# A Fourier-mixing layer and a feed-forward layer on one core: transposes through DRAM in four chunks on two queues, inverse twiddle matrices formed by TensorE, and a reordered start

## The chip, the cores and the metric

The kernel runs on one core of one Trainium2 chip. A core has TensorE (PE, matrix products into PSUM, with PEld for its weight loads), VectorE (DVE), ScalarE (ACT), GpSimd (POOL) and SyncE (SP). Here SP and POOL also issue the transfers: each has a queue that is served in order, so an issue that waits holds up everything behind it on that queue. All transfers are carried by the same 16 DMA engines. The metric is the device time of one execution in microseconds, and the number to compare is a median over runs.

## The reference

`x` has 8 batches of 3008 rows by 256 columns. Each batch is Fourier-transformed along its rows, multiplied by a complex filter, and transformed back. The result goes through a feed-forward layer of width 2048 with a leaky activation.

```python
batch, seq, dim = (8, 3008, 256)
X = np.fft.rfft(x, axis=1)
F = (filt_r + 1j * filt_i)[None, :, :]
y = np.fft.irfft(X * F, n=x.shape[1], axis=1)
...
h = x @ w_in                                      # x is now y as 24064 x 256; w_in is 256 x 2048
g = np.maximum(h, 0.0) + alpha * np.minimum(h, 0.0)
return (g @ w_out).astype(np.float32)             # w_out is 2048 x 256
```

## The kernel before

**The transform.** 3008 = 47 x 64, so the transform of a batch is done in two stages with a transpose between them, and the inverse likewise. Class `Fft` holds one batch:

- `piece_a` (16 per batch, L162): a 47-point transform of one piece of `x` (tile `xs`, loaded and cast by `load_x`, four chunks per batch, L120) by one 512-column matmul (L168); the PSUM result is copied to `asb`, by ACT (L250) or DVE (L253).
- `save_a` (4 per batch, L171) writes a quarter of `asb` to DRAM in runs of 4 KB. `turn_a` (L175), once per batch after the last save, reads it back into tile `at` with the other axis on partitions: four DMAs, each in runs of 512 bytes.
- `piece_b` (12 per batch, L184): two matmuls with matrix `twf_s` (L188), then two products on DVE with the filter, `uu` (L191) and `ww` (L192, with `filts_s`, a copy of the filter with its halves exchanged). `piece_b0` (L195) is the form for batch 0, with six matmuls and no need of `filts_s`.
- `piece_c` (12 per batch, L211): four matmuls with the inverse matrix `twi_s` (L220, L221), copied to tile `v`. `twi_s` is loaded from a constant in DRAM.
- `turn_c` (4 per batch, L224) writes a quarter of `v` to DRAM in runs of 512 bytes by four DMAs; the last call also reads all of it back into `zt` by four DMAs in runs of 4 KB.
- `piece_d` (16 per batch, L238): four matmuls (L243) and a copy into `yT`, the input of the feed-forward layer.

**The feed-forward layer.** The token axis is cut in blocks of 512 (one of 384 in every twelve). Class `Block` runs 16 steps per block. `up(j)` (L327) is two 512-column matmuls (L332) per step; after each odd step ACT copies two steps' worth from PSUM tile `hps` to `gt` (L337), and DVE finishes the activation with two scalings (`m`, L340) and one addition (L341). `down` (L344) runs for the block before: four 256-column matmuls per step (L350); ACT copies its sums to `osb` (L355), and SP stores them (L316).

**What sets the order.** Every engine's order is the order in which the program emits its instructions; nothing is reordered. First comes a prologue, in which batch 0 goes through stages a to d alone. Then a loop runs over steps, numbered from 0: `up`, `down` of the block before, and then the entries that `plan` holds for that step. Block 0 (steps 0 to 15) has no `down`. `plan_fft(b, a0, ga, ta, b0, gap, d0)` (L364) places the other batches' pieces: `piece_a` from step `a0`, every `ga` steps; `turn_a` at `ta`; `piece_b` from `b0`, every `gap` steps, with `piece_c` three steps behind it; `piece_d` from `d0`. All evictions of planned pieces are on ACT, but those of batch 0's `piece_d`, which alternate between ACT and DVE (L383).

**Buffers.** PSUM has two buffers of `hps`, two of `op` and two of `psF`; planned a, b, c and d pieces all take their bank from `psF` (function `bank`, L146). `at`, `asb`, `v` and `zt` have one buffer each, `xs` four.

**Queues before.** SP issues the constants, saves, turns and stores. POOL issues the transfers that cast: `x`, the filter, `w_in`, `w_out`. Two tiny copies into `gate` on POOL (L273, L293) hold `w_in` and `w_out` back until batch 0's `at` has landed, and the `x` of batch 1 (the second batch) until `zt` has.

Of the kernel before, what the change touches and what calls it, by code (L numbers as in the profile page):

```python
# [25 lines left out]
def _build_consts():  # L26

    s1 = np.arange(N1)
    s2 = np.arange(N2)
    k1 = np.arange(NK1)
    p = np.arange(64)
    k2 = np.where(p < 32, p, 95 - p)
    g = np.where(p < 32, 1.0, -1.0)

    a1 = 2 * np.pi * np.outer(s1, k1) / N1
    wf1 = np.zeros((2 * N1, 96))  # L40
    wi3 = np.zeros((96, 2 * N1))
    scale = np.where(k1 == 0, 1.0, 2.0) / NFFT
    for h in range(2):
        r = slice(h * N1, h * N1 + N1)
        wf1[r, h * 48 : h * 48 + NK1] = np.cos(a1)
        wf1[r, h * 48 + NK1 : h * 48 + 48] = -np.sin(a1)
        wi3[h * 48 : h * 48 + NK1, r] = (np.cos(a1) * scale).T
        wi3[h * 48 + NK1 : h * 48 + 48, r] = (-np.sin(a1) * scale).T
# [4 lines left out]
    twf = np.empty((128, NK1, 128))  # L53
    twf[:64, :, :64], twf[64:, :, :64] = c, s
    twf[:64, :, 64:], twf[64:, :, 64:] = -s * g, c * g
    ec, es = c.transpose(2, 1, 0), s.transpose(2, 1, 0)
    gp = g[:, None, None]
    twi = np.empty((128, NK1, 2, 128))
    twi[:64, :, 0, :64], twi[:64, :, 0, 64:] = ec, es
    twi[64:, :, 0] = -twi[:64, :, 0]  # L60
    twi[:64, :, 1, :64], twi[:64, :, 1, 64:] = -es * gp, ec * gp
    twi[64:, :, 1] = twi[:64, :, 1]
    return wf1, wi3, twf, twi


@with_exitstack
def kernel(
# [15 lines left out]
    twi_d = nc.inline_tensor(twi_np.astype(np.float16), name="c_twi")  # L83
# [29 lines left out]
    gate = konst.tile([128, 2], FP16, name="gate")  # L113
    yT = konst.tile([128, 2, 2 * NFFT], FP16, name="yT")

    def xrow(b, h, c):
# [35 lines left out]
    class Fft:  # L152
# [16 lines left out]
            evict(self.asb[:, 2 * i : 2 * i + 2].rearrange("p a d -> p (a d)"), ps[0:96])  # L169

        def save_a(self, c):  # L171
            s = slice(8 * c, 8 * c + 8)
            nc.sync.dma_start(out=a_dram[self.b, :, s], in_=self.asb[:, s])

        def turn_a(self, eng, ka=0, kb=NK1):  # L175
            for h in range(2):
                for c in range(2):
                    r = h * 48 + c * NK1
                    q = c * 64 + NH * h
                    eng.dma_start(  # L180
                        out=self.at[q : q + NH, ka:kb],
                        in_=a_dram[self.b, r + ka : r + kb].rearrange("k s d -> s k d"))
# [28 lines left out]
        def piece_c(self, kp, evict, pv=None):  # L211
# [9 lines left out]
                nc.tensor.matmul(pv[:, kh], twi_s[:, k1, 1], ww[:, kh], start=False, stop=True)  # L221
            evict(self.v[:, 2 * kp : 2 * kp + 2], pv)

        def turn_c(self, q):  # L224
            k = 6 * q
            for h in range(2):
                for c in range(2):
                    r = h * 48 + c * NK1 + k
                    p = c * 64 + NH * h
                    nc.sync.dma_start(  # L230
                        out=v_dram[self.b, r : r + 6].rearrange("k s d -> s k d"),
                        in_=self.v[p : p + NH, k : k + 6])
            if q == 3:
                for g in range(4):
                    s = slice(8 * g, 8 * g + 8)
                    nc.sync.dma_start(out=self.zt[:, s], in_=v_dram[self.b, :, s])
# [30 lines left out]
    nc.sync.dma_start(out=twi_s[:, 12:24], in_=twi_d.ap()[:, 12:24])  # L267
    nc.sync.dma_start(out=wi3_s, in_=wi3_d.ap())
    alp = psO.tile([128, 2, D], FP32, name="op")
    nc.tensor.transpose(alp[:, 0, 0:16], al16, id32)  # L270
    nc.vector.tensor_copy(al_s, alp[:, 0, 0:16])
    nc.gpsimd.tensor_scalar(alm_s, al_s, 1.0, -1.0, OP.mult, OP.add)
    nc.gpsimd.tensor_copy(gate[:, 0:1], f0.at[:, 11, 0:1])  # L273
    for kt in range(2):
        nc.gpsimd.dma_start(out=win_s[:, kt], in_=moe_w_in[kt * 128 : (kt + 1) * 128])
    for q in range(2):
# [4 lines left out]
    for kp in range(12):  # L281
        f0.piece_b0(kp)
        if kp >= 1:
            f0.piece_c(kp - 1, on_act, psO.tile([128, 2, D], FP32, name="op"))
        if kp >= 3 and kp % 3 == 0:
            f0.turn_c(kp // 3 - 1)
    f0.piece_c(11, on_act, psO.tile([128, 2, D], FP32, name="op"))
    f0.turn_c(3)
# [5 lines left out]
    for c in range(4):  # L294
        xc[(1, c)] = load_x(1, c)
    for i in range(4):
        f0.piece_d(i, both[i % 2], i % 2 == 1)

# [62 lines left out]
    def put(step, fn, *args):  # L361
        plan.setdefault(step, []).append((fn, args))

    def plan_fft(b, a0, ga, ta, b0, gap, d0):  # L364
        f = Fft(b)
        for i in range(16):
            put(a0 + ga * i, f.piece_a, i, on_act)
        for c in range(4):
            put(a0 + ga * (4 * c + 3), f.save_a, c)
            if b + 1 < NB:  # L370
                put(a0 + ga * (4 * c + 3) + 1,
                    lambda b=b, c=c: xc.update({(b + 1, c): load_x(b + 1, c)}))
# [62 lines left out]
```

## Time and profile before

| what | value |
|---|---|
| median of 3 runs | 861.59 us (860.19 to 862.68) |
| span of the profiled execution | 861.4 us |
| PE busy | 799.4 us (93%) |
| first 512-column matmul of batch 0's `piece_a` starts | 7.54 us |
| first matmul of `piece_b0` starts | 33.05 us |
| last matmul of batch 0's `piece_c` starts | 53.81 us |
| first matmul of `piece_d` starts | 63.08 us |
| step 0 / step 16 of the loop starts | 64.62 / 81.80 us |
| PE busy in 191.3 to 861.4 us | 657.3 of 670.1 us |

The profile shows for each engine what it did and what ended its idle time. A rows' "idle before" counts only where the engine sets the end; here that is PE for nearly all of the loop. The table says that PE has little to give after some 190 us: what it lacks to its span lies ahead of that.

### The profile page before, as it was taken

What the parts mean: (1) busy time and instruction counts of PE and PEld (TensorE: products, weight loads), DVE (VectorE), ACT (ScalarE), POOL (GpSimd) and SP (SyncE); (2) the same over time, 40 slices, a digit from 0 to 9 for tenths busy, and PEclk for the clock granted to TensorE, in tenths of its full rate; (3) what the DMA queues carried; (4) which work ended last, traced back from release to release, by engine and by line L of the source; (5) the groups of instructions that cost most, each with busy time, mean ns of one, the idle gap of its engine ahead of it and who ended that gap; (6) DMA issues with size and microseconds to landing.
All of it is one profiled execution on the core that took longest, in us unless ns stands there. A gap on an engine that the chain in (4) does not pass through costs nothing.

```text
span 861.4 us, 15404 instructions
## 1 busy us (share of the span) xinstructions
PE 799.4 (93%) x5809; PEld 541.7 (63%) x5809; DVE 612.9 (71%) x1361; ACT 586.6 (68%) x817; POOL 41.4 (5%) x85
## 2 busy tenths in 40 slices
PE   3458989979999999999999999999999999999997
PEld 1134556756666766676666766676666766676665
DVE  2246668758877787678877787778877788777773
ACT  2027757767787767777777767777777866677663
POOL 4103000000000000000000000000000000000000
PEclk9989989999999999999999999999999999999999
DMA  9989835761368224772268323682148122411111
GB/s 212 250 171 197 179 69 133 157 144 41 75 148 199 60 62 97 172 158 51 53 162 195 73 64 83 164 181 50 43 120 186 50 68 50 129 38 39 39 41 49
DMA packets 95378, 95.95 MB, mean 111 GB/s; under 512 B 8312, under 2 KB 85128, under 8 KB 95176
## 3 DMA queue, kind: packets, MB, share of 16 engines
q1 hardware_dynamic: 85448, 78.19, 35.8%
q0 software_dynamic: 8256, 16.00, 12.3%
q10 hardware_dynamic: 1600, 0.79, 0.5%
q8 instruction: 45, 0.74, 0.4%
q14 instruction: 29, 0.24, 0.1%
HBM read 59.55 MB, written 49.81 MB: 127 GB/s over the span
## 4 chain that ended last, share of the span: by engine, by line
PE 70%; DVE 13%; ACT 7%; DMA 6%; issue 2%; SPq 1%; POOL 0%; ACTq 0%; DVEq 0%; POOLq 0%
PE hps L332 29%; PE op L350 28%; ACT gt L337 6%; DVE gt L341 4%; DVE m L340 4%; PE psF L168 3%; DVE ww L192 3%; DVE uu L191 3%; PE psF L221 2%; DMA at<-a_dram 2%; PE psF L243 2%; DMA a_dram<-asb 2%; PE psF L220 1%; DMA xs<-in_x_dram 1%; PE psF L188 1%
## 5 line engine op out<-in xcount | busy, mean ns | idle before, releaser
L337 ACT ACTIVATE gt<-hps 128x1024 f16<-128x1024 f32 (+1 forms) x384 | 385.1, 1003 | 134.6 <-PE hps L332 134.1
L332 PE MATMUL hps<-yT,win_s 128*128 128x512 f16 (+1 forms) x1536 | 454.3, 377 | 1.1 <-ACT yT L250 1.0
L350 PE MATMUL op<-wout_s,gt 128*128 128x256 f16 x3008 | 453.3, 273 | 0.6 <-DVE gt L341 0.6
L350 PEld LDWEIGHTS <-gt 128*128 128x128 f16 x3008 | 294.4, 98 | 192.5 <-issue 2.8
L340 DVE TENSOR_SCALAR m<-gt,alm_s 128x512 f16<-128x512 f16 (+1 forms) x768 | 233.5, 346 | 164.1 <-ACT gt L337 162.8
L341 DVE TENSOR_TENSOR gt<-gt,m 128x1024 f16<-128x1024 f16 (+1 forms) x384 | 261.6, 681 | 24.3 <-DVE m L340 0.9
L332 PEld LDWEIGHTS <-win_s 128*128 128x128 f16 x1536 | 145.6, 98 | 31.6 <-issue 5.0
L250 ACT ACTIVATE asb<-psF 96x512 f16<-96x512 f32 x120 | 70.7, 593 | 40.2 <-PE psF L168 40.2
L250 ACT ACTIVATE v<-psF 128x512 f16<-128x512 f32 x84 | 50.2, 598 | 34.9 <-PE psF L221 34.9
L250 ACT ACTIVATE yT<-psF 128x376 f16<-128x376 f32 x120 | 58.1, 484 | 20.9 <-PE psF L243 20.7
L191 DVE TENSOR_TENSOR uu<-psF,filt_s 128x512 f16<-128x512 f32 x84 | 57.4, 683 | 6.7 <-PE psF L188 6.7
L355 ACT ACTIVATE osb<-op 128x512 f32<-128x512 f32 x96 | 56.3, 587 | 6.9 <-PE op L350 3.7
L168 PE MATMUL psF<-xs,wf_s 94*96 94x512 f16 x120 | 47.8, 398 | 11.0 <-DMA xs<-in_x_dram 8.3
L192 DVE TENSOR_TENSOR ww<-psF,filts_s 128x512 f16<-128x512 f32 x84 | 57.1, 679 | 0.0
L123 POOL DMA_DIRECT2D xs<-in_x_dram x64 | 32.9, 522 | 458.2 <-PE psF L168 457.1
L243 PE MATMUL psF<-wi_s,zt 96*128 96x94 f16 x504 | 42.7, 207 | 10.8 <-DMA zt<-v_dram 9.0
L243 PEld LDWEIGHTS <-zt 96*128 96x128 f16 x512 | 36.3, 100 | 18.9 <-DMA zt<-v_dram 9.3
L221 PE MATMUL psF<-ww,twi_s 128*128 128x256 f16 x168 | 41.1, 272 | 6.2 <-DVE ww L192 3.5
L220 PE MATMUL psF<-uu,twi_s 128*128 128x256 f16 x168 | 42.9, 272 | 1.1 <-ACT yT L250 0.5
L188 PE MATMUL psF<-at,twf_s 128*128 128x256 f16 x168 | 32.3, 274 | 8.1 <-issue 4.5
L220 PEld LDWEIGHTS <-twi_s 128*128 128x128 f16 x192 | 19.0, 99 | 18.0 <-issue 13.2
L250 ACT ACTIVATE v<-op 128x512 f16<-128x512 f32 x12 | 7.2, 597 | 32.4 <-PE op L221 32.4
(35 smaller groups left out, 130.8 us busy)
## 6 DMA issues: line engine op xcount, KB each, us to landing
out_dram<-osb SPq DMA_DIRECT2D x128, 128.0 KB
a_dram<-asb SPq DMA_DIRECT2D x32, 384.0 KB
v_dram<-v SPq DMA_DIRECT2D x128, 96.0 KB
zt<-v_dram SPq DMA_DIRECT2D x32, 384.0 KB
xs<-in_x_dram POOLq DMA_DIRECT2D x64, 188.0 KB, 5.1
at<-a_dram SPq DMA_DIRECT2D x28, 384.0 KB
twi_s<-c_twi SPq DMA_DIRECT2D x2, 768.0 KB
filts_s<-filt_s SPq DMA_DIRECT2D x2, 768.0 KB
```

The costliest lines, as they stand in the source:

```text
L168: nc.tensor.matmul(ps[0:96], wf1_s, xs[:, o : o + 512], start=True, stop=True)
L191: nc.vector.tensor_mul(uu, px, filt_s[:, 2 * kp : 2 * kp + 2])
L192: nc.vector.tensor_mul(ww, px, filts_s[:, 2 * kp : 2 * kp + 2])
L220: nc.tensor.matmul(pv[:, kh], twi_s[:, k1, 0], uu[:, kh], start=True, stop=False)
L221: nc.tensor.matmul(pv[:, kh], twi_s[:, k1, 1], ww[:, kh], start=False, stop=True)
L243: nc.tensor.matmul(ps[:, m], self.zt[:, 8 * g + 4 * mh + m, dh * 128 : dh * 128 + 128], wi3_s, start=True, stop=True)
L250: nc.scalar.activation(o, i, AF.Copy)
L332: nc.tensor.matmul(self.hps[:, j % 2, 0:tn], win_s[:, kt, j * 128 : (j + 1) * 128], yT[:, kt, self.t0 : self.t0 + tn], start=(kt == 0), st ...
L337: nc.scalar.activation(g[:, :, 0:tn], self.hps[:, :, 0:tn], AF.Copy)
L340: nc.vector.tensor_scalar(m[:, i, 0:tn], g[:, i, 0:tn], 0.0, a, OP.min, OP.mult)
L341: nc.vector.tensor_add(g[:, :, 0:tn], g[:, :, 0:tn], m[:, :, 0:tn])
L350: nc.tensor.matmul(self.op[:, si % 2], self.gts[k][:, 128 * si : 128 * si + 128], wout_s[:, k], start=(k == 0), stop=(k == 15))
```

## The change

- **`a` transpose.** `a_dram` is laid out by chunk. `save_a(c)` writes its quarter scattered, in runs of 512 bytes, still one DMA on SP. `turn_a(c)` is called for each chunk, one DMA on POOL's queue, into 32 partitions of `at`, 12 KB contiguous for each partition. The rows of `at` come in another order, and `twf` is permuted to match.
- **`v` transpose.** `save_c(q)` writes a quarter of `v` by two DMAs on SP, and `turn_c(q)` reads that quarter at once by one DMA on POOL's queue into 24 partitions of `zt`, 16 KB contiguous for each. `wf1` and `wi3` are permuted to match.
- **`twi_s`** is no longer loaded (two DMAs of 768 KB). `form_twi(kp, evict)` makes two of its 24 matrices by eight 128-column matmuls from `twf_s` and a permutation `perm_s` (64 KB, loaded) and one eviction. Six calls stand ahead of batch 0's `piece_a`, six in the loop over `piece_b0`.
- **Prologue order.** The second half of the filter is loaded after the turns; the gates are gone; `x` of batch 1 is issued right after the last `turn_c`, ahead of `w_out`; `filts_s` is loaded at steps 2 and 3 of the loop.
- **Plan.** Batch 1's `piece_a` goes from steps 10 to 25 to steps 4 to 19, with evictions alternating between ACT and DVE, and its `piece_b` from step 40 (every 3) to step 28 (every 4). Batch 2's `piece_a` moves four steps earlier. `piece_c` follows `piece_b` by four steps instead of three, and later batches' turns come earlier.

```diff
@@ _build_consts
+    cc, s8, ri, h = np.unravel_index(np.arange(128), (4, 8, 2, 2))
+    row = 64 * ri + NH * h + 8 * cc + s8
+    twf = twf.reshape(128, NK1, 128)[row]
+    perm = np.zeros((128, 2, 128))
+    perm[np.arange(128), 0, row] = 1.0
+    perm[np.arange(128), 1, row] = -1.0
...
-    a_dram = dram.tile([NB, 96, NH, D], FP16, name="a_dram")
-    v_dram = dram.tile([NB, 96, NH, D], FP16, name="v_dram")
+    a_dram = dram.tile([NB, 4, 8, 96, D], FP16, name="a_dram")
+    v_dram = dram.tile([NB, 4, 12, 64, D], FP16, name="v_dram")
...
     xc = {(0, c): load_x(0, c) for c in range(4)}
+    nc.sync.dma_start(out=perm_s, in_=perm_d.ap())
+    nc.sync.dma_start(out=twf_s[:, 0:12], in_=twf_d.ap()[:, 0:12])
     nc.sync.dma_start(out=al16, in_=moe_alpha.rearrange("(j p) -> j p", p=128))
-    nc.sync.dma_start(out=twf_s[:, 0:12], in_=twf_d.ap()[:, 0:12])
-    for ka, kb in ((0, 12), (12, 24)):
-        load_filt(filt_s, 0, filt_r, ka, kb)
-        load_filt(filt_s, 64, filt_i, ka, kb)
+    load_filt(filt_s, 0, filt_r, 0, 12)
+    load_filt(filt_s, 64, filt_i, 0, 12)
...
         def save_a(self, c):
-            s = slice(8 * c, 8 * c + 8)
-            nc.sync.dma_start(out=a_dram[self.b, :, s], in_=self.asb[:, s])
-
-        def turn_a(self, eng, ka=0, kb=NK1):
...
+            nc.sync.dma_start(
+                out=a_dram[self.b, c].rearrange("s r d -> r s d"),
+                in_=self.asb[:, 8 * c : 8 * c + 8])
+
+        def turn_a(self, c):
+            nc.gpsimd.dma_start(
+                out=self.at[32 * c : 32 * c + 32],
+                in_=a_dram[self.b, c].rearrange("s (q k) d -> (s q) k d", q=4))
...
+        def save_c(self, q):
+            for c in range(2):
+                nc.sync.dma_start(
+                    out=v_dram[self.b, q, 6 * c : 6 * c + 6].rearrange("k s d -> s k d"),
+                    in_=self.v[64 * c : 64 * c + 64, 6 * q : 6 * q + 6])
+
         def turn_c(self, q):
...
+            nc.gpsimd.dma_start(
+                out=self.zt[24 * q : 24 * q + 24],
+                in_=v_dram[self.b, q].rearrange("a (h s) d -> (a h) s d", h=2))
...
+    def form_twi(kp, evict):
+        ps = bank(True).rearrange("p (k t n) -> p k t n", k=2, t=2)
+        for kh in range(2):
+            for t in range(2):
+                for half in range(2):
+                    nc.tensor.matmul(
+                        ps[64 * half : 64 * half + 64, kh, t],
+                        twf_s[:, 2 * kp + kh, 64 * t : 64 * t + 64],
+                        perm_s[:, 1 if (t, half) == (0, 1) else 0],
+                        start=True, stop=True)
+        evict(twi_s[:, 2 * kp : 2 * kp + 2], ps)
+
     f0 = Fft(0)
+    for kp in range(6):
+        form_twi(kp, both[kp % 2])
     for i in range(16):
         f0.piece_a(i, both[i % 2], i % 2 == 1)
         if i % 4 == 3:
             f0.save_a(i // 4)
-    f0.turn_a(nc.sync, 0, 12)
-    f0.turn_a(nc.scalar, 12, 24)
-    nc.sync.dma_start(out=twi_s[:, 0:12], in_=twi_d.ap()[:, 0:12])
+            f0.turn_a(i // 4)
     nc.sync.dma_start(out=twf_s[:, 12:24], in_=twf_d.ap()[:, 12:24])
-    nc.sync.dma_start(out=twi_s[:, 12:24], in_=twi_d.ap()[:, 12:24])
...
-    nc.gpsimd.tensor_copy(gate[:, 0:1], f0.at[:, 11, 0:1])
+    load_filt(filt_s, 0, filt_r, 12, 24)
+    load_filt(filt_s, 64, filt_i, 12, 24)
     for kt in range(2):
         nc.gpsimd.dma_start(out=win_s[:, kt], in_=moe_w_in[kt * 128 : (kt + 1) * 128])
...
     for kp in range(12):
         f0.piece_b0(kp)
+        if kp < 6:
+            form_twi(kp + 6, on_act)
         if kp >= 1:
             f0.piece_c(kp - 1, on_act, psO.tile([128, 2, D], FP32, name="op"))
         if kp >= 3 and kp % 3 == 0:
+            f0.save_c(kp // 3 - 1)
             f0.turn_c(kp // 3 - 1)
...
+    f0.save_c(3)
     f0.turn_c(3)
-    for half in range(2):
-        o = 64 * half
-        nc.sync.dma_start(out=filts_s[o : o + 64], in_=filt_s[64 - o : 128 - o])
-
-    nc.gpsimd.tensor_copy(gate[0:96, 1:2], f0.zt[:, 31, 0:1])
     for c in range(4):
         xc[(1, c)] = load_x(1, c)
+    for q in range(2):
+        nc.gpsimd.dma_start(
+            out=wout_s[:, 8 * q : 8 * q + 8],
...
-    def plan_fft(b, a0, ga, ta, b0, gap, d0):
+    def plan_fft(b, a0, ga, ta, x0, b0, gap, d0, evicts=(on_act, on_act)):
         f = Fft(b)
         for i in range(16):
-            put(a0 + ga * i, f.piece_a, i, on_act)
+            put(a0 + ga * i, f.piece_a, i, evicts[i % 2])
         for c in range(4):
-            put(a0 + ga * (4 * c + 3), f.save_a, c)
+            save = a0 + ga * (4 * c + 3)
+            put(save, f.save_a, c)
+            put(max(save + 4, ta + c), f.turn_a, c)
...
-        put(ta, f.turn_a, nc.sync)
         for kp in range(12):
             put(b0 + gap * kp, f.piece_b, kp)
-            put(b0 + gap * kp + 3, f.piece_c, kp, on_act)
+            put(b0 + gap * kp + 4, f.piece_c, kp, on_act)
         for q in range(4):
-            put(b0 + gap * (3 * q + 2) + 4, f.turn_c, q)
+            save = b0 + gap * (3 * q + 2) + 5
+            put(save, f.save_c, q)
+            put(save + 4, f.turn_c, q)
...
+    for half in range(2):
+        put(2 + half, load_filts, half)
     for i in range(4, 16):
         put(i - 4, f0.piece_d, i, both[i % 2])
-    plan_fft(1, 10, 1, 26, 40, 3, 92)
-    plan_fft(2, 50, 2, 86, 104, 5, 187)
+    plan_fft(1, 4, 1, 4, 24, 28, 4, 92, both)
+    plan_fft(2, 46, 2, 74, 0, 104, 5, 187)
     for b in range(3, NB):
         p = 96 * (b - 1)
-        plan_fft(b, p - 54, 2, p - 22, p + 6, 5, p + 91)
+        plan_fft(b, p - 54, 2, p - 33, 0, p + 6, 5, p + 91)
```

More of the change, by code (lines that the diff above doesn't have):

```diff
@@ L39, in _build_consts @@
     a1 = 2 * np.pi * np.outer(s1, k1) / N1
-    wf1 = np.zeros((2 * N1, 96))
-    wi3 = np.zeros((96, 2 * N1))
-    scale = np.where(k1 == 0, 1.0, 2.0) / NFFT
+    wf1 = np.zeros((2 * N1, 2, 2, NK1))
+    wi3 = np.zeros((4, 2, 6, 2, 2 * N1))
+    scale = np.where(k1 == 0, 1.0, 2.0)[:, None] / NFFT
     for h in range(2):
         r = slice(h * N1, h * N1 + N1)
[L45 to L48, printed above, removed]
+        wf1[r, 0, h] = np.cos(a1)
+        wf1[r, 1, h] = -np.sin(a1)
+        wi3[:, 0, :, h, r] = (np.cos(a1).T * scale).reshape(4, 6, N1)
+        wi3[:, 1, :, h, r] = (-np.sin(a1).T * scale).reshape(4, 6, N1)
     kk = k1[:, None] + 47 * k2[None, :]
@@ L52, in _build_consts @@
     c, s = np.cos(ang), np.sin(ang)
[L53 to L63, printed above, removed]
+    twf = np.empty((2, 64, NK1, 128))
+    twf[0, :, :, :64], twf[1, :, :, :64] = c, s
+    twf[0, :, :, 64:], twf[1, :, :, 64:] = -s * g, c * g
+    cc, s8, ri, h = np.unravel_index(np.arange(128), (4, 8, 2, 2))
[4 more added lines that the diff above has]
+    perm[np.arange(128), 1, row] = -1.0
+    return wf1.reshape(2 * N1, 96), wi3.reshape(96, 2 * N1), twf, perm
 @with_exitstack
@@ L78 @@
     nc = tc.nc
-    wf1_np, wi3_np, twf_np, twi_np = _build_consts()
+    wf1_np, wi3_np, twf_np, perm_np = _build_consts()
     wf1_d = nc.inline_tensor(wf1_np.astype(np.float16), name="c_wf1")
@@ L82 @@
     twf_d = nc.inline_tensor(twf_np.astype(np.float16), name="c_twf")
-    twi_d = nc.inline_tensor(twi_np.astype(np.float16), name="c_twi")
+    perm_d = nc.inline_tensor(perm_np.astype(np.float16), name="c_perm")
     konst = ctx.enter_context(tc.tile_pool(name="konst", bufs=1))
@@ L104 @@
     twi_s = konst.tile([128, NK1, 2, 128], FP16, name="twi_s")
+    perm_s = konst.tile([128, 2, 128], FP16, name="perm_s")
     filt_s = konst.tile([128, NK1, D], FP16, name="filt_s")
@@ L112 @@
     wout_s = konst.tile([128, 16, D], FP16, name="wout_s")
-    gate = konst.tile([128, 2], FP16, name="gate")
     yT = konst.tile([128, 2, 2 * NFFT], FP16, name="yT")
@@ L171, in save_a @@
         def save_a(self, c):
-            s = slice(8 * c, 8 * c + 8)
-            nc.sync.dma_start(out=a_dram[self.b, :, s], in_=self.asb[:, s])
-        def turn_a(self, eng, ka=0, kb=NK1):
[L176 to L182, printed above, removed]
+            nc.sync.dma_start(
[5 more added lines that the diff above has]
+                in_=a_dram[self.b, c].rearrange("s (q k) d -> (s q) k d", q=4))
         def piece_b(self, kp):
@@ L222, in piece_c @@
             evict(self.v[:, 2 * kp : 2 * kp + 2], pv)
-        def turn_c(self, q):
[L225 to L236, printed above, removed]
+        def save_c(self, q):
[3 more added lines that the diff above has]
+                    in_=self.v[64 * c : 64 * c + 64, 6 * q : 6 * q + 6])
+        def turn_c(self, q):
+            nc.gpsimd.dma_start(
+                out=self.zt[24 * q : 24 * q + 24],
+                in_=v_dram[self.b, q].rearrange("a (h s) d -> (a h) s d", h=2))
         def piece_d(self, i, evict, wide=False):
@@ L272 @@
     nc.gpsimd.tensor_scalar(alm_s, al_s, 1.0, -1.0, OP.mult, OP.add)
-    nc.gpsimd.tensor_copy(gate[:, 0:1], f0.at[:, 11, 0:1])
+    load_filt(filt_s, 0, filt_r, 12, 24)
+    load_filt(filt_s, 64, filt_i, 12, 24)
     for kt in range(2):
         nc.gpsimd.dma_start(out=win_s[:, kt], in_=moe_w_in[kt * 128 : (kt + 1) * 128])
+    for kp in range(12):
+        f0.piece_b0(kp)
+        if kp < 6:
+            form_twi(kp + 6, on_act)
+        if kp >= 1:
+            f0.piece_c(kp - 1, on_act, psO.tile([128, 2, D], FP32, name="op"))
+        if kp >= 3 and kp % 3 == 0:
+            f0.save_c(kp // 3 - 1)
+            f0.turn_c(kp // 3 - 1)
+    f0.piece_c(11, on_act, psO.tile([128, 2, D], FP32, name="op"))
+    f0.save_c(3)
+    f0.turn_c(3)
+    for c in range(4):
+        xc[(1, c)] = load_x(1, c)
     for q in range(2):
@@ L279 @@
             in_=moe_w_out[1024 * q : 1024 * q + 1024].rearrange("(j p) d -> p j d", p=128))
[L281 to L288, printed above, removed]
-    for half in range(2):
-        o = 64 * half
-        nc.sync.dma_start(out=filts_s[o : o + 64], in_=filt_s[64 - o : 128 - o])
-    nc.gpsimd.tensor_copy(gate[0:96, 1:2], f0.zt[:, 31, 0:1])
-    for c in range(4):
-        xc[(1, c)] = load_x(1, c)
     for i in range(4):
@@ L362, in put, with load_filts @@
         plan.setdefault(step, []).append((fn, args))
-    def plan_fft(b, a0, ga, ta, b0, gap, d0):
+    def plan_fft(b, a0, ga, ta, x0, b0, gap, d0, evicts=(on_act, on_act)):
         f = Fft(b)
         for i in range(16):
-            put(a0 + ga * i, f.piece_a, i, on_act)
+            put(a0 + ga * i, f.piece_a, i, evicts[i % 2])
         for c in range(4):
-            put(a0 + ga * (4 * c + 3), f.save_a, c)
+            save = a0 + ga * (4 * c + 3)
+            put(save, f.save_a, c)
+            put(max(save + 4, ta + c), f.turn_a, c)
             if b + 1 < NB:
-                put(a0 + ga * (4 * c + 3) + 1,
+                put(max(save + 1, x0 + 4 * c),
                     lambda b=b, c=c: xc.update({(b + 1, c): load_x(b + 1, c)}))
-        put(ta, f.turn_a, nc.sync)
         for kp in range(12):
             put(b0 + gap * kp, f.piece_b, kp)
-            put(b0 + gap * kp + 3, f.piece_c, kp, on_act)
+            put(b0 + gap * kp + 4, f.piece_c, kp, on_act)
         for q in range(4):
-            put(b0 + gap * (3 * q + 2) + 4, f.turn_c, q)
+            save = b0 + gap * (3 * q + 2) + 5
+            put(save, f.save_c, q)
+            put(save + 4, f.turn_c, q)
         for i in range(16):
             put(d0 + min(i, 4) + 2 * max(i - 4, 0), f.piece_d, i, on_act)
+    def load_filts(half):
+        o = 64 * half
+        nc.sync.dma_start(out=filts_s[o : o + 64], in_=filt_s[64 - o : 128 - o])
+    for half in range(2):
+        put(2 + half, load_filts, half)
     for i in range(4, 16):
         put(i - 4, f0.piece_d, i, both[i % 2])
-    plan_fft(1, 10, 1, 26, 40, 3, 92)
-    plan_fft(2, 50, 2, 86, 104, 5, 187)
+    plan_fft(1, 4, 1, 4, 24, 28, 4, 92, both)
+    plan_fft(2, 46, 2, 74, 0, 104, 5, 187)
     for b in range(3, NB):
         p = 96 * (b - 1)
-        plan_fft(b, p - 54, 2, p - 22, p + 6, 5, p + 91)
+        plan_fft(b, p - 54, 2, p - 33, 0, p + 6, 5, p + 91)
     prev = None
```

## The prediction

> **What bounds the kernel now.** I read first the 40 slices of the page, then the busy time by stretch, then the chain of waits, and last each engine's timeline around PE's idle stretches.
>
> ```profile
> PE   3458989979999999999999999999999999999997
> DMA  9989835761368224772268323682148122411111
> ```
>
> PE is full from the tenth slice on; the 16 DMA engines are full in the first four. The gain has to come from the first 190 us. The stretches name it (us, then busy time with counts for PE, PEld, DVE, ACT, POOL, then PE's clock, DMA share, GB/s):
>
> ```profile
> 64.60:81.80 17.20, 13.94 (x86) 6.36 (x87) 11.69 (x28) 12.19 (x19) 5.28 (x11) 0.90 0.96 199
> 105.80:110.40 4.60, 0.12 (x2) 0.07 (x2) 1.17 (x3) 0.32 (x1) 0.00 (x0) 0.84 1.20 218
> 110.40:116.20 5.80, 5.80 (x24) 3.22 (x25) 2.60 (x5) 1.97 (x2) 0.00 (x0) 0.54 0.08 29
> 182.80:186.60 3.80, 0.18 (x5) 0.08 (x2) 1.28 (x3) 0.48 (x1) 0.00 (x0) 1.00 1.01 223
> ```
>
> Two stalls of 4.6 and 3.8 us: PE waits for `at` of batches 1 and 2. After the first the granted clock is about half. The chain of waits for batch 0 (start, us, what) shows the prologue as a row of transfers:
>
> ```profile
> 14.98 0.70 DVE asb L253
> 15.74 6.18 DMA a_dram<-asb
> ...
> 23.40 9.52 DMA at<-a_dram
> ...
> 56.08 2.00 DMA v_dram<-v
> 58.20 4.83 DMA zt<-v_dram
> ```
>
> PE's and DVE's timelines show two things I use below (start, duration, what, and in brackets the idle time before it with what ended it):
>
> ```profile
> 70.21 0.33 PE L243 MATMUL psF<-wi_s,zt 96*128 96x94 f16 x4 [0.59 <-DVE yT L253]
> 110.75 1.06 PE L332 MATMUL hps<-yT,win_s 128*128 128x512 f16 x2
> 116.46 0.59 PE L332 MATMUL hps<-yT,win_s 128*128 128x512 f16 x2
> 127.09 0.38 PE L168 MATMUL psF<-xs,wf_s 94*96 94x512 f16 x1 [0.47 <-ACT v L250]
> ```
> ```profile
> 69.01 0.69 DVE L341 TENSOR_TENSOR gt<-gt,m 128x1024 f16<-128x1024 f16 x1
> 69.62 0.54 DVE L253 CAST yT<-psF 128x376 f16<-128x376 f32 x1
> ```
>
> Two `up` matmuls take 1.06 us after the stall and 0.59 once the clock is back. In block 0 a `piece_d` waits for a `psF` bank that DVE frees late, since DVE's copy stands behind the activation of the same step.
>
> **1. Prologue to `piece_b0`: -4.9 us.** `form_twi` adds PE work ahead of `piece_a`. Its inputs, 64 and 384 KB on SP, are about as early as the first `x` (7.41 us): in the trace the 384 KB moved between 4 and 6 us. A 512-column matmul takes 0.43 us there, so one of 128 columns 0.107, and 6 x 8 take 5.1 us (between 2.6 at the full clock and 10.2 if a 0.106 us weight load of `twf_s` can't be hidden; I take 5.1, as L243's short matmuls hide theirs). The six evictions (0.6 to 0.69 us, two engines) keep pace. The last copy into `asb` then ends at 15.67 + 4.6 = 20.3 (5.1 less the 0.4 us that `piece_a` spent between chunks of `x`). From there one chunk is left, not the whole: 0.1 to wake SP, a scattered save priced by the last `v_dram` writes, as many 512-byte packets (768), 3.3 us from first issue to landing; 0.6 for POOL's issue; and a contiguous read of 384 KB, for which the nearest row is `x` on the same queue, 188 KB landing in 3.6 us at least, 5.6 in the median: I take 4.0, since it doesn't cast. `at` is there at 28.2 instead of 33.05. Ahead of the turns POOL's queue has only half of the filter; behind them wait the other half (first used six `kp` later, some 11 us) and `w_in` (wanted at 60). If the read took 10 us, the longest `x` row, the gain is gone.
>
> The Trainium skill speaks against this part: by "SBUF — State Buffer", section "Door 1: The DMA port swizzle", a transfer into 32 partitions reaches 8 of 16 ports, some 218 GB/s. By that an estimate for one chunk is 1.8 us of movement where all ports would need 0.9; this trace has no such read by itself. By this rule the sum would be about 1 us longer.
>
> **2. `piece_b0` to `piece_d`: +1.1 us.** Before, 33.05 to 54.1: five `kp` at 2.21 (ten 256-column matmuls at 0.213) and seven at 1.33, where DVE (0.61 + 0.72) sets the pace. Six `kp` gain eight short matmuls: 0.86 at half speed, 0.45 at full, so 3.07 or 1.54. With 10.9 us slow, as here, the phase takes 23.5; with 5.4, as after the stall at 110.4, 20.8. I take 22.2 against 21.1. From the last `v` to `piece_d` it took 54.72 to 63.08 = 8.4 us; after, 3.3 for two saves, 0.6, and 4.5 for the last 384 KB into 24 partitions: the same. Dropping the 1.5 MB `twi_s` costs and saves nothing more: the loads landed beside this phase.
>
> **3. Block 0: +9.3 us, the largest loss.** Steps 4 to 11 now hold a `piece_d` and a `piece_a`, and both of an odd step are copied by DVE. With two `psF` banks, both are then held by copies that stand on DVE behind the activation. Per pair of steps, from the end of an odd `up`: ACT 0.1 + 1.02 (L337), DVE 0.65 + 0.65 for `m` and the addition, 0.54 for `yT`: bank free at 3.1 (the trace: `up` ended at 67.0, the copy at 70.16). Then `piece_d` runs; the second bank comes 0.65 later; `piece_a` 0.22, the next odd `up` 0.43, plus some 0.1 of hand-over: 4.5 us per pair. Before, it was 1.95 (L332 at 68.13, 70.38, 72.08, 74.08). From step 0: four steps 4.4, as before; to the end of `up` 5, 2.7; three such pairs 13.5; steps 12 to 15 out of the last wait, 5.9. Sum 26.5, against 17.2. If the copies only had to fit DVE's sum (2.33 per pair) it would be 18.4; with a half clock more than 26.5 (rival). I take 26.5: the order of DVE is written out and the copy row shows it waiting.
>
> **4. Work moved: -1.3 us.** Six `piece_a` (0.218 each) leave steps 16 to 25, where PE is full, for block 0, where it isn't.
>
> **5. First stall: -7.3, and +2.5.** The stall of 4.6 and the slow clock after it (110.4 to 115.8, half speed: 2.7) go. Now `piece_b` is at step 28. The last `piece_a` is in step 19, on DVE: its copy ends 3.2 us after that `up`, 6.9 after step 16 begins; save 3.3, issue 0.6, read 4.0 make 14.8. Step 28's `piece_b` is due 4 x 1.09 + 9 x 0.87 = 12.2 after step 16. So PE waits 2.5 us (between 0 and 5; above 3.6 the clock falls again, 2.7 more). SP has no store ahead of that save: the first comes at step 24. On POOL, `x` of batch 1 and `w_out` are issued before it, and 1.5 and 1.0 MB of these beside 1.5 MB of `filts_s` need 20 us of DMA at the 200 GB/s of that stretch; block 0 hides them. `w_out` behind `x` lands some 22 us after the last turn (8 for `x`, 14.1 its longest row); it is wanted at step 16, over 26 later.
>
> **6. Second stall: -5.5 us.** 3.8, and half of the 3.5 us slow behind it. There SP's save had stood behind `zt` reads that waited for their own writes; those now wait on POOL. Batch 2's last turn has over 20 steps to spare.
>
> **7. `psF` between pieces: +1.6 us.** Where c, b and a meet in a step, a waits 0.4 (five times before); with b every 4 steps and a every 2 they meet eight times, 0.45 each. Later batches: zero; waits for `ww` ahead of `piece_c` (0.3 us, twelve times) may go, and `b` one step behind `c` may wait as much. From -2 to +2.
>
> The Trainium skill has a second objection: by the same page, "SBUF: two separate sides", DVE in some modes keeps GpSimd from writing the descriptors of its transfers. The trace disagrees: POOL's issues took 505 ns in the median, 582 at most, between 130 and 600 us, while DVE ran L340. By that rule every turn could be late by a DVE instruction, some 0.6 us.
>
> **Sum**, against the profile's own 861.4 (0.2 under the median): -4.9 + 1.1 + 9.3 - 1.3 - 7.3 + 2.5 - 5.5 + 1.6 = -4.5, so 856.9, say **857**, with 851 to 862 as this case's own range.
>
> **Rivals.**
> - **The clock falls in block 0 (slower).** PE would be busy about 37% there, with gaps of some 2.2 us. The granted clock, 0.93 in 56 to 58 us and 0.50 in the next two, fell some 3.6 us after the matmuls ended at 54.1. If it falls in steps 5 to 12, each pair costs 0.8 more (3.3), the loop starts its full part at half speed (2.7), and the wait at step 28 lets it fall again (4). 867. Against: in steps 0 to 9, 75% busy, it stayed up. It decides once a gap passes 3.6 us.
> - **Block 0 doesn't lock.** If copies overlap as their sum allows, 8.1 us less: 849. For: PE waited only 0.3 to 0.6 us there before.
> - **Prologue bound by transfers.** DMA share is over 1.0 from 4 to 34 us. If batch 0's `at` lands no earlier than 33, 4.9 is lost: 862, no change. Against: 1,536 filter packets at some 70 ns over 16 engines, 6.7 us, move out of the way.
>
> **Chances.** Forecast 0.45, clock 0.20, no lock 0.20, transfers 0.15. A measurement tells 0.3% (2.6 us) from nothing: faster is below 859.0, slower above 864.2. Of the forecast's share 0.3 lies faster, 0.13 same, 0.02 slower; no lock 0.19 and 0.01; transfers 0.04, 0.08, 0.03; clock 0.0, 0.03, 0.17. Sum: 0.53, 0.25, 0.22. The range, 846 to 867, takes in the second and third rivals and the edge of the first.
>
> **What would show it.** `piece_b0` near 28 us; `piece_d` near 59; step 16 some 26 us after step 0, with PE waits for DVE `yT` and `asb` of over 2 us; a wait for `at` near step 28 of 2 to 3 us; none near 180; a clock of 1.0 through block 0. I am wrong if step 16 comes under 20 us after step 0, or if the turns on POOL take over 6 us.

## The result, and the profile after

The changed kernel took 871.66 us (median of 4 runs, 871.09 to 872.79), the kernel before 861.25 in the same comparison: a ratio of 1.0124, 95% interval 1.0104 to 1.0145. The prediction was 857, with a range of 846 to 867; it had the sign wrong. The profiled execution spans 869.9 us, 8.5 more than the one before.

The busy time by stretch of the changed kernel (us; then busy time with counts for PE, PEld, DVE, ACT, POOL; PE's clock, DMA share, GB/s) is cut near `piece_b0`, the last copy of `v`, `piece_d` and the steps 0 and 16:

```profile
32.40:55.00 22.60, 21.43 (x168) 11.86 (x168) 15.47 (x24) 10.28 (x18) 0.78 (x2) 1.00 0.63 124
55.00:76.20 21.20, 0.00 (x1) 0.03 (x2) 0.00 (x0) 0.29 (x1) 4.77 (x10) 0.58 0.97 175
77.70:106.20 28.50, 20.73 (x93) 9.21 (x94) 15.38 (x33) 13.95 (x21) 1.99 (x3) 0.68 0.58 104
200.00:800.00 600.00, 598.50 (x4515) 417.97 (x4515) 469.90 (x1052) 454.69 (x640) 39.16 (x76) 1.00 0.43 102
```

The second row is the loss: for 21.2 us no engine computes, and the DMA engines are busy 97% of it. The third is block 0: step 16 begins at 105.82, 28.1 us after step 0, where it had been 17.2. The fourth is a gain: the same row of the kernel before has PE busy for 593.03 us of the 600.

```profile
200.00:800.00 600.00, 593.03 (x4420) 410.30 (x4418) 459.95 (x1035) 444.10 (x621) 16.28 (x32) 1.00 0.43 101
```

The chain of waits through the prologue (start, us, what), to be held against that of before:

```profile
17.88 0.70 DVE asb L247
...
18.65 5.11 DMA a_dram<-asb
...
24.27 8.00 DMA at<-a_dram
...
55.93 9.81 DMA v_dram<-v
...
66.28 0.49 POOL zt L228
```

The last save of `v` takes 9.81 us from there to its landing; the same row of before had 2.00. POOL can issue the read only at 66.28, and PE's timeline (start, duration, what, idle time before it) shows when that landed, and which later waits are left:

```profile
76.20 0.47 PE L237 MATMUL psF<-wi_s,zt 96*128 96x94 f16 x4 [21.54 <-DMA zt<-v_dram]
121.67 0.38 PE L185 MATMUL psF<-at,twf_s 128*128 128x256 f16 x2 [3.33 <-DMA at<-a_dram]
194.52 0.33 PE L237 MATMUL psF<-wi_s,zt 96*128 96x94 f16 x4 [2.74 <-DMA zt<-v_dram]
```

The stalls for `at` of before (4.6 and 3.8 us) have become one of 3.3, and a new one of 2.7 for batch 1's `zt` at step 92.

What SP did in the meantime is in its timeline, first of the changed kernel, then of the kernel before:

```profile
42.82 14.91 SPq L223 DMA_DIRECT2D v_dram<-v  x8
57.85 1.40 SPq L392 DMA_DIRECT2D filts_s<-filt_s  x2
```
```profile
58.20 1.72 SPq L236 DMA_DIRECT2D zt<-v_dram  x4
60.08 1.19 SPq L291 DMA_DIRECT2D filts_s<-filt_s  x2
```

`filts_s` is planned for steps 2 and 3, which PE reached after 80 us. SP issued it at 57.85, 0.1 us after it had issued the last save; before, it stood behind the reads of `zt`, which waited for that save to land. A place in the plan is a place in an engine's order; SP had nothing in front of these two issues to wait for.

| from | to | before | after | difference | predicted |
|---|---|---|---|---|---|
| start | `piece_b0` | 33.05 | 32.41 | -0.6 | -4.9 |
| `piece_b0` | `piece_d` | 30.03 | 43.79 | +13.8 | +1.1 |
| step 0 | step 16 | 17.2 | 28.1 | +10.9 | +9.3 |
| step 16 | end | 779.6 | 764.1 | -15.5 | -10.0 |
| sum | | | | +8.5 | -4.5 |

The predicted -10.0 is the sum of steps 4 to 7. `piece_d` to step 0 took 1.5 us in both. A step begins with the first matmul of its `up`.

### The profile page after: what moved, and what is told of

Same layout as the page of the kernel before. It is cut to its first block, busy times and chain, and to the rows that moved or that the text cites. A ratio compares the mean times of both kernels' runs of the same rounds, so it can differ in the third digit from the quotient of the medians.

```text
span 869.9 us, 15584 instructions
## 1 busy us (share of the span) xinstructions
PE 801.3 (92%) x5905; PEld 548.7 (63%) x5905; DVE 621.2 (71%) x1372; ACT 589.7 (68%) x818; POOL 73.6 (8%) x147
## 4 chain that ended last, share of the span: by engine, by line
PE 86%; DMA 7%; ACT 3%; issue 2%; DVE 2%; SPq 0%; POOL 0%; ACTq 0%; POOLq 0%; DVEq 0%
PE op L355 36%; PE hps L337 36%; PE psF L168 4%; PE psF L237 2%; PE psF L218 2%; PE psF L185 2%; DMA v_dram<-v 2%; PE psF L217 2%; DMA at<-a_dram 1%; DMA xs<-in_x_dram 1%; ACT gt L342 1%; DMA a_dram<-asb 1%; ACT v L244 1%; PE hps L200 1%; DMA zt<-v_dram 1%
## 5 line engine op out<-in xcount | busy, mean ns | idle before, releaser
L337 PEld LDWEIGHTS <-win_s 128*128 128x128 f16 x1536 | 145.9, 99 | 38.7 <-issue 12.5
L244 ACT ACTIVATE asb<-psF 96x512 f16<-96x512 f32 x112 | 66.2, 591 | 40.2 <-PE psF L168 40.2
L237 PE MATMUL psF<-wi_s,zt 96*128 96x94 f16 x504 | 43.5, 210 | 28.9 <-DMA zt<-v_dram 24.3
L228 POOL DMA_DIRECT2D zt<-v_dram x32 | 16.5, 515 | 464.3 <-DMA v_dram<-v 235.8
L177 POOL DMA_DIRECT2D at<-a_dram x32 | 16.2, 508 | 158.1 <-DMA a_dram<-asb 130.6
## 6 DMA issues: line engine op xcount, KB each, us to landing
win_s<-in_moe_w_in_dram POOLq DMA_DIRECT2D x2, 512.0 KB, 11.2
```

The costliest lines, as they stand in the source:

```text
L237: nc.tensor.matmul(ps[:, m], self.zt[:, 8 * g + 4 * mh + m, dh * 128 : dh * 128 + 128], wi3_s, start=True, stop=True)
L244: nc.scalar.activation(o, i, AF.Copy)
L337: nc.tensor.matmul(self.hps[:, j % 2, 0:tn], win_s[:, kt, j * 128 : (j + 1) * 128], yT[:, kt, self.t0 : self.t0 + tn], start=(kt == 0), st ...
```

## The experiments

For the 13.8 us stood a theory and two rivals. **Theory:** the 1.5 MB of `filts_s`, let loose early, take the DMA engines from the last save and the last read. **Rivals:** the scattered save by two DMAs on SP is slow by itself; or the `x` and `w_out` issued right behind the read crowd it. For block 0: the copies on DVE lock `psF`, against a fallen clock or late data. For the gain after 200 us: the fourth step between `piece_b` and `piece_c`, against the new queues.

**1. filts_s later.**

```diff
-        put(2 + half, load_filts, half)
+        put(8 + half, load_filts, half)
```

> The changed kernel with the two loads of filts_s (1.5 MB) put at steps 8 and 9 instead of 2 and 3, so that on SP they stand behind a save that waits, and are not issued right behind the last two saves of batch 0's v. Theory (transfers crowd each other): the last save of v, 9.8 us in the changed kernel, falls to 3 to 4.5 us, the read into zt behind it falls a little too, and the loop starts 6 to 9 us sooner; total 863 to 866. Rival (a save scattered in runs of 512 bytes is slow by itself): the save stays at 9 to 10 us and the total at 870 to 872.

864.44 us (ratio to before 1.0032, interval 1.0018 to 1.0046), 7.2 less than the changed kernel. At steps 8 and 9 SP's order holds them behind a save of batch 1, so they wait. The chain:

```profile
54.85 4.21 DMA v_dram<-v
59.59 5.34 DMA zt<-v_dram
```

9.81 became 4.21, and the read 5.3 instead of 9.8, with `x` still issued right behind it. SP issues `filts_s` at 82.37. `piece_d` starts at 65.02, and step 0 at 66.54, 11.2 us sooner; 8.4 of that are left at step 93, behind a longer block 0 and slower steps after step 28. The theory holds for both transfers. How far the save falls differs from kernel to kernel: experiment 9 comes back to it.

**2. x held back by a gate, filts_s as in the change.**

```diff
+    nc.gpsimd.tensor_copy(gate[0:96, 1:2], f0.zt[:, 31, 0:1])
     for c in range(4):
         xc[(1, c)] = load_x(1, c)
```

(`gate` is a small tile that is made for this.)

> The changed kernel with one tiny copy on POOL, ahead of the loads of batch 1's x and w_out, that reads zt and so holds these loads back until batch 0's zt has landed. Theory (transfers issued right behind a read slow it): the last read into zt, 9.9 us, falls to 5 to 7 us and piece_d starts 3 to 5 us sooner; part of it comes back as waits for x near step 4; total 866 to 870. Rival (a read of 384 KB into 24 partitions from POOL's queue takes 10 us by itself): it stays at 9 to 10 us, x is 5 us later, total 871 to 877.

871.2 us (1.0111, 1.0092 to 1.013): nothing gained. Its chain:

```profile
54.20 9.24 DMA v_dram<-v
63.98 8.82 DMA zt<-v_dram
```

With nothing behind the read but `filts_s` in flight, both stay long; the read is 1.0 us shorter, where the theory of this run asked for 3 to 5. `piece_d` starts at 72.89, 3.3 us sooner, 1.7 of it since the save was issued sooner, but at step 93 nothing of it is left (194.71 against 194.68). The `x` behind the read was not what made it long.

**3. Batch 1's `piece_a` copied by ACT alone.**

```diff
-    plan_fft(1, 4, 1, 4, 24, 28, 4, 92, both)
+    plan_fft(1, 4, 1, 4, 24, 28, 4, 92)
```

> The changed kernel with all evictions of batch 1's piece_a on ACT instead of alternating between ACT and DVE. Theory (both psF banks of an odd step are held by DVE behind the activation): steps 0 to 16 take 18 to 20 us instead of 28.5, the waits of PE for yT and asb on DVE in steps 6 to 12 go, total 861 to 865; the wait for at near step 28 may grow by up to 5 us, since less time stands ahead of it, which would leave 864 to 868. Rival (the block is held by x or by the clock): 26 us or more stay, total 868 to 872.

862.7 us (1.0019, 1.0003 to 1.0035), 9.0 less than the changed kernel, though `piece_d` still comes at 76.71. Block 0 runs from 78.2 to 99.7, 21.5 us instead of 28.1; 18 to 20 had been expected. The wait for `at` at step 28, which might have grown, fell to 1.4 us. What went is this, in the changed kernel's PE and DVE timelines:

```profile
87.82 0.33 PE L237 MATMUL psF<-wi_s,zt 96*128 96x94 f16 x4 [1.63 <-DVE yT L247]
92.22 0.47 PE L237 MATMUL psF<-wi_s,zt 96*128 96x94 f16 x4 [1.31 <-DVE yT L247]
97.20 0.33 PE L237 MATMUL psF<-wi_s,zt 96*128 96x94 f16 x4 [1.35 <-DVE yT L247]
```
```profile
90.36 0.62 DVE L345 TENSOR_SCALAR m<-gt,alm_s 128x512 f16<-128x512 f16 x2 [2.00 <-ACT gt L342]
91.02 0.69 DVE L346 TENSOR_TENSOR gt<-gt,m 128x1024 f16<-128x1024 f16 x1
91.62 0.54 DVE L247 CAST yT<-psF 128x376 f16<-128x376 f32 x1
92.08 0.68 DVE L247 CAST asb<-psF 96x512 f16<-96x512 f32 x1
```

Both `psF` banks wait for `yT` and `asb`, which stand on DVE behind `m` and `gt`, and these wait 2 us for ACT, whose input is the `up` that PE could not start earlier. It is a ring: PE, ACT, DVE, PE, and the spacing of the waits (4.40 and 4.98 us) is its length for two steps.

**4. piece_c three steps behind again.**

```diff
-            put(b0 + gap * kp + 4, f.piece_c, kp, on_act)
+            put(b0 + gap * kp + 3, f.piece_c, kp, on_act)
```

> The changed kernel with piece_c three steps behind piece_b, as before, instead of four. Theory (the fourth step is what took PE's small waits out of the stretch after 200 us): PE's busy share in 200 to 800 us falls from 99.8% to 98.8% and the total grows by 5 to 9 us, to 877 to 880. Rival (the new queues and layouts of the turns did it): no change, 870 to 873.

880.05 us (1.0216, 1.0192 to 1.0239), 8.4 more than the changed kernel; PE is busy 592.34 of the 600 us. The loss grows by 1.4 to 2.3 us with every 96 steps, that is with every batch. The mechanism can be seen in the kernel before, first PE, then DVE:

```profile
511.01 0.27 PE L220 MATMUL psF<-uu,twi_s 128*128 128x256 f16 x1
511.60 0.27 PE L221 MATMUL psF<-ww,twi_s 128*128 128x256 f16 x1 [0.32 <-DVE ww L192]
```
```profile
509.65 0.69 DVE L341 TENSOR_TENSOR gt<-gt,m 128x1024 f16<-128x1024 f16 x1
510.26 0.68 DVE L191 TENSOR_TENSOR uu<-psF,filt_s 128x512 f16<-128x512 f32 x1
510.86 0.68 DVE L192 TENSOR_TENSOR ww<-psF,filts_s 128x512 f16<-128x512 f32 x1
```

`uu` and `ww` stand behind the activation of an odd step, so the second matmul starts 0.59 us after the first, where 0.11 is the distance without a wait (125.36 and 125.47 in the changed kernel): `ww` comes 0.5 us late. The rows' labelled waits (twelve of 0.3 us) add up to less than half of what the fourth step gives back, since most late starts are hidden by the first matmul's modelled end. The distances between starts show the whole: from step 110 to the end, those from a `uu` matmul to its `ww` matmul sum to 27.0 us in the kernel before and 27.3 in this one, 15.5 in the changed kernel and in experiment 5. The stretch itself takes 668.2 us in the kernel before and in this one, 657.0 in the changed kernel and 657.5 in experiment 5. So nothing of the 11 us is left for the new queues, the rival.

**5. The fourth step in the kernel before, and nothing else.** The same line of the kernel before, `+ 3` to `+ 4`.

> The kernel before, with one number changed: piece_c follows piece_b by four steps instead of three. Theory (piece_c's matmuls waited for ww, which stands on DVE behind m and gt of the same step; a fourth step takes some 2 us out of each batch from batch 2 on, and out of batch 1 as well): 861.4 less 8 to 10, so 851 to 853, TensorE busy some 6 us more of the stretch from 200 to 800 us. Rival (the fourth step only pays together with the change's other parts, pieces a beside b and turns in chunks): within 2 us of 861. No other row of the first 190 us should move by more than 1 us.

853.01 us, before 862.19 beside it: 0.9907 (0.9879 to 0.9936), PE busy 598.93 of 600. One digit gives 9.2 us without any other part of the change. The rest of the change therefore costs 871.7 - 853.0, some 19 us. The expectation that no row of the first 190 us moves by more than 1 us did not come true: in this profile step 0 begins at 60.97 instead of 64.62, and block 0 takes 19.1 us instead of 17.2. The edit does not touch the prologue, so 3.7 us of it are scatter between two profiles.

**6. Experiments 1 and 3 together; 7 and 8. The filter's second half and `w_in` held behind `at`.** The sixth has both edits above. The seventh is experiment 1, the eighth the sixth, each with

```diff
+    nc.gpsimd.tensor_copy(gate[:, 0:1], f0.at[:, 11, 0:1])
     load_filt(filt_s, 0, filt_r, 12, 24)
```

> The changed kernel with two edits: filts_s loaded at steps 8 and 9, and batch 1's piece_a copied by ACT alone. Apart they gave -7.2 and -8.9 against 871.6. If they are independent: 855.5, step 0 near 66.5, step 16 near 88, the wait for at of batch 1 not above 3.4. Rival (with block 0 short again, the 1.5 MB of filts_s at steps 8 and 9 now stand beside batch 1's saves and its second block, so the wait for at grows and the clock behind it falls): 859 to 862, with a wait for at of 5 us or more.

> The changed kernel with filts_s at steps 8 and 9 (864.4 by itself), and the filter's second half and w_in held back by a tiny copy that reads the last chunk of at. If the 7 to 8 us of the last read of at come from these transfers beside it: the read falls to about 5, piece_b0 starts 2 to 3 us earlier (29.5 to 30.5), and 861.5 to 862.5 comes out, if the second half of the filter still lands before the seventh piece_b0. Rival (the read is slow by itself, since it goes into 32 partitions, or beside the three reads before it): 7 to 8 us as before, 864 or, where the late filter is now waited for, up to 867.

> All three edits in the changed kernel: filts_s at steps 8 and 9, batch 1's piece_a copied by ACT alone, and the gate ahead of the filter's second half and w_in. If the parts add, 855.5 less 2 to 3: 853. If the gate gives nothing, as the other kernel of this call without it. If the late filter is waited for, 1 to 4 us above that kernel.

The sixth: 856.85 us (0.9955, 0.9935 to 0.9975); the sum of the parts was 855.5, and its wait for `at` is 3.04. The parts are nearly independent, though step 0 (69.75) and step 16 (91.22) come 3 us later than expected, the last save taking 6.84 us here. The gate gave nothing: 864.24 against 864.44 and 856.44 against 856.85, with the last read of `at` at 9.30 us in the one profile and 5.66 in the other. The filter and `w_in` are not what makes this read long. What is beside it is its own kind: the DMA queues of the eighth kernel between 26 and 28 us, with nothing of the filter's second half issued yet (packets, MB, share of 16 engines):

```profile
q0 software_dynamic: 55, 0.44, 99.2%
q1 hardware_dynamic: 42, 0.01, 2.8%
```

POOL's queue alone, that is the chunk reads, fills the engines with 0.44 MB in 2 us, 220 GB/s. In the changed kernel the four of them are issued between 18.5 and 24.3 us and land at 25.3, 28.9, 30.6 and 32.3, so the last is served behind the ones before. The Trainium skill ("SBUF — State Buffer", "Door 1: The DMA port swizzle") gives some 218 GB/s as the bound for a transfer into 32 partitions; the row's 220 is near it, but up to three reads into different partitions are in flight there, so it is no test of that bound.

**9. The read of `v`'s third quarter held behind the last save.** On the sixth kernel:

```diff
-            f0.turn_c(kp // 3 - 1)
+            if kp < 9:
+                f0.turn_c(kp // 3 - 1)
...
+    nc.gpsimd.dma_start(out=gate[0:2, 0:2], in_=v_dram[0, 3, 5:7, 0, 0:2])
+    f0.turn_c(2)
     f0.turn_c(3)
```

> The changed kernel with filts_s at steps 8 and 9 and batch 1's piece_a on ACT (856.9; its last save of v took 6.8 us), with one more edit: in batch 0 the read of v's third quarter into zt is held on POOL's queue by a tiny read of v_dram that waits for the last save, so that no read stands beside that save. Theory (the read's 12 and 16 KB packets hold the DMA engines that the save's 512-byte packets need): the save takes 2 to 3.5 us; the two reads then move 768 KB together at some 210 GB/s and take 5 to 8 us; the time is 855 to 858. Rival (two transfers out of 64 partitions each are slow by themselves, where before there were four out of 32): the save still takes 5 to 7 us, piece_d comes 2 us or more later, and the time is 859 or more.

858.85 us (0.9977, 0.9958 to 0.9997), 2.0 more than the sixth kernel, though the two intervals overlap; it lies between the theory's range and the rival's. The save took 4.23 us in its profile (that of its fastest run), between the two expectations; without the edit it took 6.84, 6.38, 6.94 and 7.04 in four kernels with late `filts_s`, but 4.21 in experiment 1. So a chunk read beside the save is not shown to be what stretches it, and what the hold may give the save, the two reads take back: from the last copy of `v` to `piece_d` it is 13.9 us here and 13.6 in the sixth kernel. Why the save takes up to 7 us without `filts_s` stays open.

**10. The kernel before with piece_b later.** On experiment 5:

```diff
-    plan_fft(1, 10, 1, 26, 40, 3, 92)
-    plan_fft(2, 50, 2, 86, 104, 5, 187)
+    plan_fft(1, 10, 1, 26, 44, 3, 92)
+    plan_fft(2, 50, 2, 86, 108, 5, 187)
```

> The kernel before with piece_c four steps behind (853.0 by itself), and piece_b of batches 1 and 2 four steps later (from steps 44 and 108). Theory: the two stalls for at (4.7 and 3.8 us) were a matter of when the step stands in the plan, not of how fast the transposes are; four steps are some 7 us of other work for TensorE. Both go, and the slow clock behind them (2.7 and some 1.8) with them: 840 to 844. Rival (the wait moves on to zt of batch 1, due at step 92, as in the changed kernel): one stall of 2 to 4 us near 180 us stays, 845 to 849.

847.5 us (0.9832, 0.9799 to 0.9865): the rival's number, and the rival's wait. PE's timeline:

```profile
111.08 0.38 PE L188 MATMUL psF<-at,twf_s 128*128 128x256 f16 x2 [1.24 <-issue]
170.11 0.34 PE L243 MATMUL psF<-wi_s,zt 96*128 96x94 f16 x4 [2.86 <-DMA zt<-v_dram]
```

The wait for `at` shrank from 4.7 to 1.2 (labelled `issue`, as that of before is), that of batch 2 is gone, but `zt` of batch 1, due at step 92, is now late.

**11. The same room in the changed kernel.** On the sixth:

```diff
-    plan_fft(1, 4, 1, 4, 24, 28, 4, 92)
+    plan_fft(1, 4, 1, 4, 24, 32, 3, 92)
```

> The changed kernel with filts_s at steps 8 and 9 and batch 1's piece_a on ACT (856.9 by itself), and batch 1's piece_b from step 32, every 3 steps, instead of from 28, every 4. Theory: its two remaining stalls, for at at step 28 (3.0) and for zt at step 92 (3.7), both go, since the first b has four steps more and the last c comes seven steps earlier: 856.9 less 6.7 and up to 2 us of slow clock, 848 to 850.5. Rival (pieces b and c every 3 steps make psF banks wait more, or the wait for at stays): 852 to 856.

848.75 us (0.9842, 0.981 to 0.9873). Both waits are gone from its PE timeline, as expected, so behind the start the chunked transposes leave no wait of PE over 1 us. The start is what this kernel lacks: step 16 begins at 92.50, against 82.29 in experiment 10.

**12. The kernel before, with batch 1's pieces b and c packed.** On the tenth:

```diff
-            put(b0 + gap * kp, f.piece_b, kp)
+            put(b0 + int(gap * kp), f.piece_b, kp)
...
-    plan_fft(1, 10, 1, 26, 44, 3, 92)
+    plan_fft(1, 10, 1, 26, 46, 2.5, 92)
```

`piece_c` and `turn_c` follow with the same rounding.

> The kernel before with piece_c four steps behind and batch 2's piece_b from step 108 (with batch 1's from 44 every 3 steps, 847.5, two waits of TensorE left: 1.2 us for at at step 44 and 2.9 for zt at step 92), and now batch 1's piece_b from step 46, every 2 and 3 steps in turn. Theory (both waits are a matter of the step): the first b comes two steps, some 3 us, later, and the last turn_c six steps, some 9 us, earlier; both waits go, 842.5 to 844.5. Rival (at 2.5 steps the pieces b and c fill DVE and the two psF banks, so that up or the pieces a wait instead): 846 to 849.

840.63 us (839.37 to 841.2), before 860.5 beside it: 0.9763, interval 0.9735 to 0.979, the fastest of all, 19.9 us below the kernel before and 2 below the expected range. Both waits are gone. The longest waits left on PE from 60 us on are the prologue's for `zt` and one for `x`:

```profile
60.62 0.49 PE L243 MATMUL psF<-wi_s,zt 96*128 96x94 f16 x4 [9.12 <-DMA zt<-v_dram]
75.47 0.39 PE L168 MATMUL psF<-xs,wf_s 94*96 94x512 f16 x1 [1.99 <-DMA xs<-in_x_dram]
```

It keeps the transposes, the queues and the prologue of before, and changes only the steps at which pieces b and c stand.

## Why the prediction was wrong, point by point

**Step 1, the prologue: gain mis-sized, -0.6 instead of -4.9.** The copies into `asb` ended at 18.6, even earlier than the 20.3 predicted. The save took 5.1 instead of 3.3 and the read 8.0 instead of 4.0. The step priced the last chunk as if it stood alone. The two reads before it, and the second half of `twf_s`, were still moving. The objection that was put at 1 us, 32 partitions at half rate, has a rate near the row's 220 GB/s, but it was applied to one chunk where three stood in a row. The named rival, a prologue bound by transfers, describes this part, and the remark that the filter's packets move out of the way missed what fills their place. Of the prediction's own signs of being wrong, one came: the turns on POOL took over 6 us.

**Step 2 is where the prediction failed.** The phase of `piece_b0` and `piece_c` took 22.2 us to the end of its last matmul, as predicted. But "from the last `v` to `piece_d` ... the same", 8.4 us, became 20.9 (55.30 to 76.20): 12.5 us, nearly all of the 13.0 by which the sum was off. The step did not ask what SP issues next. With `filts_s` late the stretch takes 10.8 to 13.8 us in five kernels, so 7 to 10 of the 12.5 us are the crowding by `filts_s`; in the measured time, late `filts_s` gave 7.2. The other 2.4 to 5.4 us are a save and a read that were priced too low even so: 4.2 to 7.0 and 5.3 to 5.5 us, where the step put 3.3 and 4.5. Before, `filts_s` was issued behind `zt` reads that themselves waited for the saves. With these reads moved to POOL, nothing on SP waited any more. The working of step 5 placed `filts_s` beside batch 1's `x`, by its step in the plan and not by SP's order.

**Step 3, block 0: right in mechanism, 28.1 against 26.5.** The ring on DVE was there, with a spacing of 4.4 us where 4.5 was predicted, and taking it away gave 6.6 us of block and 9 of time. PE's waits in it were 1.3 to 1.8 us, not over 2. The forecast's clock of 1.0 was wrong: it was 0.68 on average, at 0.50 to some 82 us, as the kernel before has it to 68 us, and then again from some 89 to 96 and from some 99 to 106. The rival "the clock falls in block 0" came true along with the forecast, but at another condition: no wait of PE there is longer than 1.8 us, where the rival named a gap of 3.6. The slow clock shows as one spacing of 4.98 us instead of 4.40 and as slow `up` matmuls (1.06 us) behind 101.6, and it can account for the 1.6 us that are missing; of the rival's further 6.7 there is little, since two `up` matmuls take 0.59 to 0.60 us again from 107.1 on. In experiment 3, with the ring gone, the clock is 0.90, low only to some 82 us.

**Steps 4 to 6.** The stalls for `at` went as predicted, and the wait at step 28 was 3.3 us (2.5 predicted, 0 to 5 as bounds) with the clock at 1.00 behind it. Not foreseen was the wait for batch 1's `zt` at step 92, 2.7 us: its last read is issued at step 81, four steps after the last save, where the kernel before issued it at step 77; the clock fell behind it, and steps 92 to 104 took 4.5 us more than before. Against that, steps 16 to 92 gave 3.4 us (4.5 predicted) and steps 104 to 110, the second stall, 5.4 (5.5 predicted). From step 16 to 110 the kernel gained 4.3 us, where steps 4 to 7 had put 10.

**Step 7: sized at zero, worth 8 to 9 us.** The waits for `psF` came (seven or eight of 0.47). The "zero, from -2 to +2" for the later batches is the second large miss, with the other sign: 8.4 us are lost by taking the fourth step out, 9.2 gained by putting it into the kernel before, and the profiles show 11.2 from step 110 to the end. The step read the labelled waits, 12 of 0.3 us, as the whole price, and allowed for no more than that. PE's 593 busy us in 600 of the profile before had shown 7 us of gaps there; the front table's 657 of 670 was read as "little to give".

The objection in step 7, that DVE delays POOL's issues, showed no sign in the times of the issues: in the changed kernel 36 of 80 issues between 130 and 600 us overlap a DVE `m`, with a median of 512 ns against 510 for the others. The 40 issues on which the prediction rested had only 4 such.

In sum: 12.7 us between `piece_b0` and `piece_d`, 4.3 from step 1, 1.6 from block 0, less 5.5 after step 16, make the 13.0 between -4.5 and +8.5, but for 0.1 of rounding in the parts.

## What to carry to other kernels

An issue that waits is also a brake for what stands behind it on its queue: whoever moves the wait to another queue must ask what the first queue will now send, and when. A chunked transpose puts its own reads beside its own writes, so its last chunk is to be priced with the earlier ones in flight. Before a transfer is made faster, it is cheaper to try the consumer at a later step: here later steps gave 20 us to the old kernel (9 of them for DVE's `ww`, the rest for transfers), and no kernel with the chunked transposes came below 848.75 us. Which part of the change costs what in the start, beyond `filts_s` and the copies on DVE, was not taken apart.

## What the runs showed of the hardware

- A 1.5 MB load issued 2 us behind a 384 KB scattered save on the same queue stretched that save to 9.2 to 10.1 us in four kernels (4.2 to 7.0 in five with the load elsewhere), and the read on POOL's queue to 8.8 to 10.1 (5.3 to 5.5 in those five). The Trainium skill says that DMAs from different engines run on the same 16 DMA engines and interleave ("DMA: Bandwidth & Descriptors", "Issuing engines are not separate DMA queues"); these runs agree.
- The granted clock averaged 0.63 from 90 to 98 us and 0.58 from 98 to 106.2, in block 0, with PE busy 62% and 77% of the time and no wait longer than 1.8 us; behind the 3.3 us wait at step 28 it stayed at 1.00, behind the 2.7 us at step 92 it fell to 0.50. The Trainium skill ("TensorE: Matmul & The Clock Gate", "A second HAM failure mode: psum-queue depth-cycling") tells of a clock that goes up and down from short idle times between groups of matmuls; this trace has both, and that the cause is the same is not shown.
- The same read of `at`, in kernels with the same prologue up to it, took from 6.2 to 11.0 us in eight profiles, and `piece_b0` started between 31.0 and 33.7. One profile does not tell 2 us of such a transfer from none.
